# A changed prologue for a fused attention and expert kernel: scores first, block sums of v as products of their own, loads and splits in a new order

## The chip, the cores and the metric

The kernel runs on one core of a Trainium2 chip. The metric is the device time of one execution in microseconds, the median of several executions. TensorE (PE) multiplies matrices; its weight loads are listed as PEld. VectorE (DVE), ScalarE (ACT) and GpSimd (POOL) do elementwise work, and SyncE (SP) issues nearly all DMA transfers. Each engine takes its own instructions strictly in the order in which they were written.

## The reference

Three layers follow one another. The first is attention: 2 batches, 8 heads, 768 positions, head size 64. Each query sees the keys within 15 positions of itself and, beside them, 24 block keys, each the maximum over 32 keys; the value of a block is the mean of its 32 values.

```python
k_sum = k.reshape(B, H, nb, block, D).max(axis=3)
v_sum = v.reshape(B, H, nb, block, D).mean(axis=3)
scores_l = scale * np.matmul(q, k.transpose(0, 1, 3, 2))
scores_s = scale * np.einsum('bhsd,bhnd->bhsn', q, k_sum) + np.log(block)
scores_all = np.concatenate([np.where(mask_l, scores_l, -1e9), scores_s], axis=-1)
a = softmax(scores_all)
x = np.matmul(a, np.concatenate([v, v_sum], axis=2))
```

The second is a dense layer on 1536 tokens, `g = elu(x @ w_in)` and `x2 = g @ w_out`, with 512 and 2048 columns. The third is a top-1 mixture of 8 experts on `x2`, each with 512, 1024 and 512 columns and a limit on its number of tokens.

## The kernel before

The tokens are cut into four parts of 384 (`t` = 0 to 3, called NT). For attention a *pair* `p` is one part with two heads, 16 pairs in all, and a *unit* `u` is half a pair, 192 queries. The loop over `sl` writes one *slot* per unit; inside a slot the engines' work is written by hand, and that order is final, for there is no scheduler behind it. In slot `sl` the kernel writes the scores of unit `u = sl` (`pe_s`, tile S), the masked maximum (`dve_max`, custom DVE instructions on S), the exponential (`act_exp`), the division (`norm`: two small DVE instructions, L290 and L291, and a product on POOL), the transpose of unit `u-1` (`pe_t`, tile T), and the output of unit `u-2` (`pe_o`, tile O). Between them `busy(n)` writes n transposes of the identity matrix into an unused tile, called *fillers* here (tile `warm`).

The scores need the window keys `kw`. `prep_k` makes them from the loaded keys `kt`: two copies of key columns (the main one of 64 columns per window, the rest of 32), a maximum over blocks (`ks`, L195) and a copy of `ks`. The block sums of v are reduced on DVE from `vt` (`prep_va`, L209), transposed by PE (`pe_va`, tile V), scaled by ACT into `vs` (`fin_va`) and brought by a DMA of their own (`load_vs`) below the 96 window rows of `vw`, so that `pe_o` multiplies 120 rows at once. `pe_va` of the next pair is written before the scores of that pair.

Nine slots come before the dense layer sets in (`LAG` is 9). Slot 8 (`LAG - 1`) is a special one: it holds the scores of unit 8 and the first two products h0 and h1 of the first part with `w_in`, three of their four row blocks before the last outputs of attention are there and the fourth after them. Slots 9 to 16, called n = 0 to 7 here, each hold one attention unit of part 1 and one pair of products (tile h with `w_in`, tile acc with `w_out`) of part 0. For part 0 the weights are used as whole 32-bit numbers, put together by three DVE instructions each (`w_conv`, L399, L403, L406); for later parts they are split in two: `w_split` writes a rounded copy on ACT and the remainder on POOL (L413). `wpend` lists the splits that are due, `split_next()` takes one. From slot 18 on attention and the dense layer go on in another branch that the change does not touch. After the dense layer comes the routing to experts, and then the experts.

The sets `splits` (i0, i1, i2, o0, i3, o1, ... o7) and `corder` say in which order weights are loaded, put together and split. SP takes all loads from one list, and a load whose buffer is still in use holds up what stands behind it.

Of the kernel before, what the change touches and what calls it, by code (L numbers as in the profile page):

```python
# [9 lines left out]
F32 = mybir.dt.float32  # L10
# [10 lines left out]
P = 128  # L21
# [28 lines left out]
def build(tc, cap, qT, kT, vT, vP, wi, wo, wg, wgT, wx, out):  # L50
# [6 lines left out]
    with ctx:  # L57
# [111 lines left out]
        def load_vt(p):  # L169
            t, pr = divmod(p, NPAIR)  # L170
            if t % 2 == 0:
                if p == NPAIR - 1:
                    VT[p] = xpool.tile([P, NPAIR, S], F32, tag="xT2", name=f"vt{p}")[:, 0]
                else:
                    VT[p] = apool.tile([P, S], F32, tag="vt", bufs=1, name=f"vt{p}")
                nc.sync.dma_start(VT[p], vT[t // 2, pr])

        def load_vw(p):
            t, pr = divmod(p, NPAIR)
            b, half = divmod(t, 2)  # L180
            vw = apool.tile([P, QPT, P], F32, tag="vw", name=f"vw{p}")
            vbase = (b * (S + 2 * WIN) + half * TT) * DM + pr * P
            nc.sync.dma_start(
                vw[0:WK], bass.AP(vP.tensor, vbase, [[DM, WK], [QB * DM, QPT], [1, P]]))
            VW[p] = vw

        def prep_k(p):

            t, pr = divmod(p, NPAIR)
            kt = KT[p]  # L190
            kw = apool.tile([P, QPT, KEYS], F32, tag="kw", name=f"kw{p}")
            KW[p] = kw
            if t % 2 == 0:
                KS[p] = apool.tile([P, NSUM], F32, tag=f"ks{pr}", bufs=1, name=f"ks{p}")
                nc.vector.tensor_reduce(  # L195
                    out=KS[p], in_=kt[:, WIN : WIN + S].rearrange("p (u s) -> p u s", s=BLK),
                    op=ALU.max, axis=AX.X)
            else:
                KS[p] = KS[p - NPAIR]
            (nc.vector.tensor_copy if p >= 3 * NPAIR else nc.scalar.copy)(kw[:, :, 0:QB], kt[:, 0:TT].rearrange("p (i k) -> p i k", k=QB))  # L200
            rest = nc.gpsimd.tensor_copy if t == 0 and pr else nc.scalar.copy if t == 1 else nc.vector.tensor_copy
            rest(kw[:, :, QB:WK], kt[:, QB : QB + TT].rearrange("p (i k) -> p i k", k=QB)[:, :, 0 : WK - QB])
            (nc.gpsimd if t == 0 and pr else nc.vector).tensor_copy(
                out=kw[:, :, WK:KEYS], in_=KS[p].unsqueeze(1).to_broadcast([P, QPT, NSUM]))
# [21 lines left out]

        def load_vs(p):
            nc.sync.dma_start(
                out=VW[p][WK:KEYS], in_=VS[p][WK:KEYS].unsqueeze(1).to_broadcast([NSUM, QPT, P]))
# [75 lines left out]
        def pe_o(u):  # L305
            p, t, pr, g0 = where(u)
            po = PS["o", u] = psm(f"O{u}", "O")
            pT = PTS.pop(u)
            for gi in range(GRP):
                for hh in range(2):  # L310
                    nc.tensor.matmul(
                        po[hh * D : (hh + 1) * D, gi * QB : (gi + 1) * QB],
                        lhsT=VW[p][0:KEYS, g0 + gi, hh * D : (hh + 1) * D],
                        rhs=pT[0:KEYS, gi, hh * QB : (hh + 1) * QB], start=True, stop=True)

# [554 lines left out]
        load_k(0)  # L870
        load_q(0)
        load_vt(0)
        load_k(1)
        load_q(1)
        load_vw(0)
        prep_k(0)
        prep_va(0)
        pe_va(0)
        load_vt(1)
        load_vw(1)  # L880


# [51 lines left out]
        for sl in range(total):  # L934
# [16 lines left out]
            cv = list(corder.get(sl, ())) if sl >= LAG else []  # L951
            if 0 < n < FPG - 2:
                wpend.append(splits[n - 1])
            if FPG - 2 <= n <= FPG:
                wpend.extend(splits[2 * n - FPG + 1 : 2 * n - FPG + 3])
            if FPG < n < 2 * FPG - 2:
                wpend.append(splits[n + 2])

# [13 lines left out]
            if sl == LAG - 1:  # L972
# [4 lines left out]
                pe_o(u - 2)  # L977
                act_o(u - 2)
                w_conv([("i", 2)], (0, 1))
                pe_t(u - 1)  # L980
                mm1(0, 1, range(NCC - 1))
                w_conv([("i", 2)], (2,))
                w_prefetch()
                act_t(u - 1)
                pe_o(u - 1)
                act_o(u - 1)
# [3 lines left out]
                load_vs(p)  # L990
                load_k(p + 2)
                dve_max(u)
                elu_exp(0, 0)
                elu_max(0, 0)
                act_exp(u)
                prep_k(p + 1)
                norm(u)
                continue
# [157 lines left out]
            if u < NU:  # L1156
                pe_s(u)
            if sl < LAG - 1:
                busy(2 if sl < LAG - 3 else 4)
            if u - 2 in late:  # L1160
# [5 lines left out]
            if u < NU and sl % GPP == (p == 0):  # L1166
                fin_va(p)
                load_vs(p)
            if u < NU and sl % GPP == 0:
                if p + 2 < NPR:  # L1170
                    load_k(p + 2)
                if p + 2 == NPAIR - 1:
                    load_vt(p + 2)
            if u < NU and sl % GPP == 1 and p + 2 < NPR:
                load_q(p + 2)
            if u < NU and sl % GPP == 1 and p and p + 1 < NPR:
                load_vw(p + 1)
            if el:
                elu_exp(*el[1:])
            if u < NU:  # L1180
                dve_max(u)
                act_exp(u)

            if el:
# [3 lines left out]
            if dense:  # L1188
# [3 lines left out]
                split_next()  # L1192
                if n >= FPG - 2:
                    split_next()
                if sl % GPP and p + 1 < NPR:
# [12 lines left out]
            if u < NU and sl % GPP == 1 and p + 1 < NPR:  # L1208
                if not dense:
                    prep_va(p + 1)  # L1210
                if p + 2 < NPR and p + 2 != NPAIR - 1:
                    load_vt(p + 2)
            if sl < LAG and u - 2 in late:
                dve_o(u - 2)
            if u < NU and not dense:
                norm(u)
            if sl in (LAG - 3, LAG - 2):
                w_conv([("i", sl - LAG + 3)])
                w_prefetch()
# [16 lines left out]
            conv_next()  # L1236
            if sl in (LAG - 6, LAG - 5, LAG - 4, LAG - 3):
                w_prefetch()
            if sl < LAG - 1:
                busy(2 if sl < LAG - 3 else 4)  # L1240
            if 0 <= u - 1 < NU and u != NU:
# [115 lines left out]
        for v in range(3):  # L1357
            nc.vector.tensor_reduce(
                out=tabs[:, :, v].rearrange("p (k j) -> p k j", j=nj), in_=tmp[v], op=ALU.add, axis=AX.X)
            if v == 0:  # L1360
                by_rank(2)
        ysf = bpool.tile([P, DM], F32, tag="ys", bufs=3, name="ysf")
        busy(4)
        ahead(0, GRP)
        allsl = slots(tabs, NE * nj, "1")
        for k in range(1, NE):
            GS[k] = allsl + (k * nj,)
        finish(blk.y, st["slot0"][0][:, 0:1], st["slot0"][1][:, 0:1], "f", ysf)

# [105 lines left out]
def _layout(np, q, k, v, moe_w_in, moe_w_out, moe2_w_gate, moe2_w1, moe2_w2):  # L1475
# [4 lines left out]
    vT = v.reshape(NB, NPAIR, 2, S, D).transpose(0, 1, 2, 4, 3).reshape(NB, NPAIR, P, S)  # L1480
    vP = np.pad(v.transpose(0, 2, 1, 3).reshape(NB, S, DM), ((0, 0), (WIN, WIN), (0, 0)))
    wi = moe_w_in.reshape(NCC, P, NFC, P).transpose(2, 1, 0, 3).reshape(NFC, P, 512)
    wo = moe_w_out.reshape(NFC, P, DM)
# [24 lines left out]
```

## Time and profile before

| | before |
|---|---|
| median of 3 runs | 500.39 us (499.85 to 500.6) |
| the profiled execution, own time | 502.35 us |
| its span, first to last instruction | 500.6 us |
| PE busy | 473.9 us, 95% of the span |
| PEld, DVE, ACT, POOL busy | 394.3, 336.2, 265.3, 184.4 us |
| moved by DMA | 73.15 MB, mean 146 GB/s |
| DMA share in the first 44 us | 0.91 |

The profile shows one execution, with times from the start of its span. A busy PE isn't a PE at its peak, since matmuls are pipelined and their ends are modelled; so lengths of PE work are read here from the start of one group to the start of the next. [...] The chain of waits of this profile covers only the last microsecond, so the stretches are read from the order of time instead.

### The profile page before, as it was taken

The numbers are of one execution on the slowest core, as the hardware profiler recorded it, in microseconds if no ns is written. First come the engines' busy times: TensorE is split into PE (matmuls) and PEld (weight loads), VectorE is DVE, ScalarE is ACT, GpSimd is POOL, SyncE is SP. The second block draws the span as 40 slices with busy tenths as digits, with TensorE's granted clock in tenths as the row PEclk, the third lists the DMA queues.
The fourth block names the chain that finished last, engine by engine and source line by source line (L and its number), as shares of the span: only waits on it lengthen the run. The fifth ranks groups of instructions, "written<-read, shape, count | busy, mean of one in ns | idle before, by whom it ended". The sixth has DMA issues, their size and how long they took to land. (4 is left out here: it accounts for less than half of the span.)

```text
span 500.6 us, 9042 instructions
## 1 busy us (share of the span) xinstructions
PE 473.9 (95%) x2996; PEld 394.3 (79%) x2996; DVE 336.2 (67%) x887; ACT 265.3 (53%) x666; POOL 184.4 (37%) x189
## 2 busy tenths in 40 slices
PE   7999998899999999999999999999998999999892
PEld 6665555588888899998999999889768889888681
DVE  3778999866666557887179889747695855365560
ACT  3846556577665655564333333434735856476450
POOL 4412435665333347886333233122524030120340
PEclk8999999999999999999999999999999999999898
DMA  7898784332433253479010010105536875376470
GB/s 226 255 278 221 223 250 135 92 111 76 135 106 94 57 184 104 147 264 321 5 63 2 0 64 1 64 0 191 151 122 215 300 234 184 125 237 190 160 243 14
DMA packets 41890, 73.15 MB, mean 146 GB/s; under 512 B 4188, under 2 KB 18780, under 8 KB 41808
## 3 DMA queue, kind: packets, MB, share of 16 engines
q1 hardware_dynamic: 40048, 67.01, 43.2%
q0 software_dynamic: 1760, 5.19, 3.4%
q8 instruction: 34, 0.56, 0.5%
q14 instruction: 48, 0.39, 0.3%
HBM read 61.88 MB, written 9.70 MB: 143 GB/s over the span
## 5 line engine op out<-in xcount | busy, mean ns | idle before, releaser
L430 PE MATMUL h<-xT,Wi 128*128 128x384 f32 x672 | 130.2, 340 | 0.0
L475 PE MATMUL acc<-Wo,g 128*128 128x512 f32 x504 | 127.3, 396 | 0.6 <-POOL g L455 0.6
L430 PEld LDWEIGHTS h<-xT,Wi 128*128 128x128 f32 x672 | 118.0, 188 | 5.8 <-issue 1.9
L455 POOL TENSOR_TENSOR g<-e,g 128x384 fp32r<-128x384 f32 x55 | 65.0, 1182 | 131.5 <-ACT g L449 131.5
L475 PEld LDWEIGHTS acc<-Wo,g 128*128 128x128 f32 x504 | 92.8, 188 | 18.6 <-POOL g L455 1.4
L442 DVE SCALAR_TENSOR_TENSOR e<-e,h 128x384 f32<-128x384 f32 x64 | 35.3, 552 | 51.1 <-ACT e L438 48.8
L437 ACT ACTIVATE e<-h 128x384 f32<-128x384 f32 x64 | 31.5, 492 | 57.7 <-PE h L430 54.0
L667 DVE TENSOR_TENSOR E<-rawq,E 128x512 fp32r<-128x512 f32 x70 | 47.8, 723 | 9.6 <-ACT E L657 8.4
L449 ACT CAST g<-e 128x384 fp32r<-128x384 f32 x56 | 28.8, 514 | 45.7 <-DVE e L442 45.7
L284 ACT ACTIVATE sc<-sc,st 128x120 f32<-128x120 f32 x96 | 36.7, 385 | 20.1 <-DVE st L277 20.0
L799 PE MATMUL bh<-xbq,E 128*128 128x256 f32 (+1 forms) x288 | 43.6, 303 | 3.2 <-ACT ysf L703 1.3
L799 PEld LDWEIGHTS bh<-xbq,E 128*128 128x128 f32 x288 | 41.2, 188 | 5.5 <-issue 1.5
L657 ACT CAST E<-rawq 128x512 fp32r<-128x512 f32 x75 | 42.3, 617 | 4.5 <-issue 2.5
L292 POOL TENSOR_TENSOR sc<-sc,st 128x360 f32<-128x360 f32 x32 | 27.6, 862 | 43.6 <-DVE st L291 26.3
L788 PE MATMUL y<-E,g 128*128 128x512 f32 x168 | 41.7, 393 | 0.0
L537 DVE CUSTOM_DVE_ANT_0 dot<-a,wgb 128x512 f32<-128x512 f32 x48 | 40.0, 888 | 0.0
L788 PEld LDWEIGHTS y<-E,g 128*128 128x128 f32 x168 | 30.6, 188 | 5.7
L438 ACT ACTIVATE e<-e 128x384 f32<-128x384 f32 x64 | 33.6, 526 | 2.0
L277 DVE CUSTOM_DVE_ANT_0 sc<-S,masks 128x120 f32<-128x120 f32 x96 | 21.4, 277 | 17.9 <-PE S L252 11.0
L303 ACT COPY pT<-T 120x384 f32<-120x384 f32 x32 | 15.3, 480 | 26.8 <-PE T L299 25.5
L807 DVE TENSOR_TENSOR g<-e,g 128x256 fp32r<-128x256 f32 (+1 forms) x24 | 11.3, 470 | 24.7 <-ACT g L806 24.7
L704 POOL DMA_INDIRECT out<-ys,sidx x6 | 6.3, 1051 | 48.0 <-ACT ys L703 46.5
(249 smaller groups left out, 702.0 us busy)
## 6 DMA issues: line engine op xcount, KB each, us to landing
rawq<-wx SPq DMA_DIRECT2D x88, 256.0 KB, 3.7
rawi<-wi SPq DMA_DIRECT2D x16, 512.0 KB, 6.4
rawo<-wo SPq DMA_DIRECT2D x16, 512.0 KB, 4.3
vw<-vP SPq DMA_DIRECT2D x16, 288.0 KB, 4.1
kt<-kT SPq DMA_DIRECT2D x8, 400.0 KB, 5.4
qt<-qT SPq DMA_DIRECT2D x16, 192.0 KB, 4.2
vt<-vT SPq DMA_DIRECT2D x8, 384.0 KB, 3.2
out<-xg SPq DMA_DIRECT2D x12, 256.0 KB, 4.4
```

The source lines that it names most:

```text
L284: nc.scalar.activation(out=sc[:, gi], in_=sc[:, gi], func=AF.Exp, bias=st[:, 0, gi : gi + 1], scale=-1.0, accum_out=st[:, 1, gi : gi + 1])
L430: nc.tensor.matmul(HP[t, f][:, 0:TT], lhsT=w[:, s, c * P : (c + 1) * P], rhs=xT[t][:, xs, c, :], start=c == 0 and n == 0, stop=c == NCC - ...
L437: nc.scalar.activation(out=e, in_=HP[t, f][:, 0:TT], func=AF.Exp)
L438: nc.scalar.activation(out=e, in_=e, func=AF.Relu, bias=1.0, scale=-1.0)
L442: nc.vector.scalar_tensor_tensor(out=e, in0=e, scalar=-1.0, in1=h[:, 0:TT], op0=ALU.mult, op1=ALU.max)
L455: eng.tensor_tensor(g[:, 1], EP.pop((t, f)), g[:, 0].bitcast(F32), op=ALU.subtract)
L475: nc.tensor.matmul(accp[tb], lhsT=g[:, s, tb * P : (tb + 1) * P], rhs=w[:, ws], start=f % FPG == 0 and n == 0, stop=f % FPG == FPG - 1 and ...
L537: nc.vector.tensor_tensor_reduce(out=junk, in0=x2[t * BPT + tb], in1=WGB[e // 2][:, e % 2], scale=1.0, scalar=0.0, op0=ALU.mult, op1=ALU.a ...
L657: (nc.vector.tensor_copy if m in vec else nc.scalar.copy)(EW[k][m][:, 0], raw_of(k, m))
L667: (nc.gpsimd if m in pool else nc.vector).tensor_tensor(w[:, 1], raw, w[:, 0].bitcast(F32), op=ALU.subtract)
L788: nc.tensor.matmul(ys[b], lhsT=g[:, s, b * P : (b + 1) * P], rhs=w[:, ws], start=f == 0 and n == 0, stop=f == 7 and n == 2)
L799: nc.tensor.matmul(h[:, 0:nt], lhsT=EW[k][half * NCC + c][:, ws, fc * P : (fc + 1) * P], rhs=xb[:, s, c, 0:nt], start=n == 0, stop=n == 3 ...
```

## The change

The program differs in eight places. The scores of pair 0 no longer stand behind the transpose of its block sums: `prep_va(0)` and `pe_va(0)` move into slots 0 and 1. For part 0 the block sums become two products of their own (24 rows, 192 columns) that open each sum in `pe_o`, and the DMA `load_vs` falls away there. `vw` is loaded from a host layout with one row of 3 KB per key instead of six of 512 bytes. The loads of keys, queries and values are issued in another order, and v of pairs 1 to 3 gets buffers of its own. The main key copies of pairs 1 to 3 move from ACT to POOL. Fillers become fewer. In slot 8 the maximum, exponential and division of unit 8 move ahead of h1. The splits are taken one per slot through n = 7 and two in n = 8 and 9. Near the end, `finish` of the first expert block moves ahead of four fillers.

```diff
@@ load_vw @@
-            vbase = (b * (S + 2 * WIN) + half * TT) * DM + pr * P
-            nc.sync.dma_start(
-                vw[0:WK], bass.AP(vP.tensor, vbase, [[DM, WK], [QB * DM, QPT], [1, P]]))
+            nc.sync.dma_start(vw[0:WK], vP[b, half, pr])
@@ prep_k @@
-            (nc.vector.tensor_copy if p >= 3 * NPAIR else nc.scalar.copy)(kw[:, :, 0:QB], kt[:, 0:TT].rearrange("p (i k) -> p i k", k=QB))
+            main = nc.gpsimd.tensor_copy if t == 0 and pr else nc.vector.tensor_copy if t == 3 else nc.scalar.copy
+            main(kw[:, :, 0:QB], kt[:, 0:TT].rearrange("p (i k) -> p i k", k=QB))
@@ load_vs @@
+            if p < NPAIR:
+                return
@@ pe_o @@
+            own = KEYS if t else WK
+            if t == 0:
+                for hh in range(2):
+                    nc.tensor.matmul(
+                        po[hh * D : (hh + 1) * D, 0 : GRP * QB],
+                        lhsT=VS[p][WK:KEYS, hh * D : (hh + 1) * D],
+                        rhs=pT[WK:KEYS, :, hh * QB : (hh + 1) * QB], start=True, stop=False)
...
-                        lhsT=VW[p][0:KEYS, g0 + gi, hh * D : (hh + 1) * D],
-                        rhs=pT[0:KEYS, gi, hh * QB : (hh + 1) * QB], start=True, stop=True)
+                        lhsT=VW[p][0:own, g0 + gi, hh * D : (hh + 1) * D],
+                        rhs=pT[0:own, gi, hh * QB : (hh + 1) * QB], start=t > 0, stop=t > 0 or gi == GRP - 1)
@@ before the loop @@
         load_k(0)
         load_q(0)
+        prep_k(0)
+        load_k(1)
         load_vt(0)
-        load_k(1)
+        load_vw(0)
         load_q(1)
-        load_vw(0)
-        prep_k(0)
-        prep_va(0)
-        pe_va(0)
         load_vt(1)
-        load_vw(1)
+        load_k(2)
@@ the splits that are due @@
-            if 0 < n < FPG - 2:
+            if 0 < n < FPG:
                 wpend.append(splits[n - 1])
-            if FPG - 2 <= n <= FPG:
-                wpend.extend(splits[2 * n - FPG + 1 : 2 * n - FPG + 3])
-            if FPG < n < 2 * FPG - 2:
-                wpend.append(splits[n + 2])
+            if FPG <= n < FPG + 2:
+                wpend.extend(splits[2 * n - FPG - 1 : 2 * n - FPG + 1])
+            if FPG + 2 <= n < 2 * FPG - 1:
+                wpend.append(splits[n + 1])
...
-                if n >= FPG - 2:
-                    split_next()
@@ slot 8 @@
+                dve_max(u)
                 w_conv([("i", 2)], (0, 1))
...
+                act_exp(u)
+                norm(u)
                 pe_o(u - 1)
...
-                load_k(p + 2)
-                dve_max(u)
                 elu_exp(0, 0)
                 elu_max(0, 0)
-                act_exp(u)
                 prep_k(p + 1)
-                norm(u)
@@ slots 0 to 7 @@
+            if sl == 1:
+                pe_va(0)
             if sl < LAG - 1:
-                busy(2 if sl < LAG - 3 else 4)
+                busy(1 if sl < LAG - 3 else 2)
...
+            if sl < LAG - 1 and sl % GPP == 1:
+                load_k(p + 3)
+                if p + 3 < NPAIR:
+                    load_vt(p + 3)
...
+            if sl == 0:
+                prep_va(0)
+            if sl in (LAG - 3, LAG - 2):
+                w_conv([("i", sl - LAG + 3)], (0, 1))
...
-            if sl < LAG - 1:
-                busy(2 if sl < LAG - 3 else 4)
+            if LAG - 3 <= sl < LAG - 1:
+                busy(2)
@@ first expert block @@
+        finish(blk.y, st["slot0"][0][:, 0:1], st["slot0"][1][:, 0:1], "f", ysf)
         busy(4)
         ahead(0, GRP)
...
-        finish(blk.y, st["slot0"][0][:, 0:1], st["slot0"][1][:, 0:1], "f", ysf)
```

On PE the start of the program stood thus before (a name's number tells one buffer from another; `x24` merges equal instructions; S is a unit's scores, V a transposed block sum, T a transposed unit, O an output):

```order
L867 MATMUL warm<-ident 128x128 x24
L217 MATMUL V_176<-ident,va_126 120x128
L263 MATMUL S_182<-kw_169,qt_159 64x120 x6
L867 MATMUL warm<-ident 128x128 x4
L263 MATMUL S_214<-kw_169,qt_159 64x120 x6
L867 MATMUL warm<-ident 128x128 x4
L299 MATMUL T_246<-ident,sc_194 120x128 x3
L217 MATMUL V_250<-ident,va_128 120x128
L263 MATMUL S_252<-kw_202,qt_165 64x120 x6
L867 MATMUL warm<-ident 128x128 x2
L311 MATMUL O_264<-pT_262,vw_167 64x64 x6
```

In the changed program the same stretch reads:

```order
L877 MATMUL warm<-ident 128x128 x24
L266 MATMUL S_179<-kw_161,qt_159 64x120 x6
L877 MATMUL warm<-ident 128x128
L266 MATMUL S_209<-kw_161,qt_159 64x120 x6
L218 MATMUL V_216<-ident,va_126 120x128
L877 MATMUL warm<-ident 128x128
L302 MATMUL T_239<-ident,sc_188 120x128 x3
L218 MATMUL V_243<-ident,va_128 120x128
L266 MATMUL S_245<-kw_197,qt_173 64x120 x6
L877 MATMUL warm<-ident 128x128
L315 MATMUL O_256<-pT_254,vs_220 64x192 x2
L321 MATMUL O_256<-pT_254,vw_171 64x64 x6
```

The first V now stands behind the scores of units 0 and 1; the second V still stands ahead of the scores of unit 2; each output has two products of 192 columns more.

On DVE the start of the changed program reads as follows (`ks` is a block maximum of keys, `va` a block sum of v, the ISA rows on `sc` are a unit's maximum and those on `st` alone its read-out; unit 0 is `sc_188`, unit 1 `sc_227`):

```order
L280 ISA st_189 128x1
L210 TENSOR_REDUCE va_126<-vt_169 128x24
L195 TENSOR_REDUCE ks_198<-kt_167 128x24
L293 TENSOR_SCALAR st_189<-st_189 128x3
L294 RECIPROCAL st_189<-st_189 128x3
L280 ISA sc_227,st_228<-S_209,masks 128x120
L280 ISA st_228 128x1
L280 ISA sc_227,st_228<-S_209,masks 128x120
L280 ISA st_228 128x1
L280 ISA sc_227,st_228<-S_209,masks 128x120
L280 ISA st_228 128x1
L210 TENSOR_REDUCE va_128<-vt_175 128x24
```

The first block sum moved from ahead of the first maximum to behind it, so that from there two sums, a key maximum, a division and a maximum stand in one row ahead of the second V.

On POOL slots n = 5 to n = 8 stood thus before (a row on `sc` is a unit's division and comes once a slot, a row on `Wi` or `Wo` is a split):

```order
L413 TENSOR_TENSOR Wi_964<-T_493,Wi_964 128x512
L292 TENSOR_TENSOR sc_954<-sc_954,st_955 128x360
L413 TENSOR_TENSOR Wo_1025<-T_493,Wo_1025 128x512
L413 TENSOR_TENSOR Wi_1028<-T_494,Wi_1028 128x512
L292 TENSOR_TENSOR sc_1015<-sc_1015,st_1016 128x360
L413 TENSOR_TENSOR Wo_1084<-T_494,Wo_1084 128x512
L413 TENSOR_TENSOR Wi_1087<-T_495,Wi_1087 128x512
L292 TENSOR_TENSOR sc_1074<-sc_1074,st_1075 128x360
L413 TENSOR_TENSOR Wo_1126<-T_495,Wo_1126 128x512
L292 TENSOR_TENSOR sc_1133<-sc_1133,st_1134 128x360
L413 TENSOR_TENSOR Wi_1158<-T_496,Wi_1158 128x512
```

In the changed program they read:

```order
L423 TENSOR_TENSOR Wi_942<-T_463,Wi_942 128x512
L295 TENSOR_TENSOR sc_932<-sc_932,st_933 128x360
L423 TENSOR_TENSOR Wo_1003<-T_463,Wo_1003 128x512
L295 TENSOR_TENSOR sc_993<-sc_993,st_994 128x360
L423 TENSOR_TENSOR Wi_1059<-T_464,Wi_1059 128x512
L295 TENSOR_TENSOR sc_1049<-sc_1049,st_1050 128x360
L423 TENSOR_TENSOR Wo_1098<-T_464,Wo_1098 128x512
L295 TENSOR_TENSOR sc_1105<-sc_1105,st_1106 128x360
L423 TENSOR_TENSOR Wi_1130<-T_465,Wi_1130 128x512
```

Slots n = 6 and n = 7 have one split each instead of two, and the two that moved stand in later slots.

## Rows read from the trace of the kernel before

**Rows 1.** Busy time per stretch (windows): stretch, length, each engine's busy us, PEclk, DMA, GB/s.

```profile
100.00:200.00 100.00, 100.00 (x784) 87.82 (x783) 62.92 (x192) 64.12 (x185) 45.66 (x43) 1.00 0.36 109
```

**Rows 2.** Waits of PE over the span: who, for whom, us in total, times, longest.

```profile
PE acc L471 <- DVE x L406: 2.6, 2, 1.5
PE O L311 <- DMA vw<-vs: 0.5, 1, 0.5
PE acc L471 <- DVE T L406: 0.2, 1, 0.2
```

**Rows 3.** Timeline of the start: start us, length us, engine, line, operation, [idle <-releaser].

```profile
1.75 4.35 PE L867 MATMUL warm<-ident 128*128 128x128 f32 x24 [1.75 <-POOL ident masks.py:199]
...
5.10 0.34 DVE L203 COPY kw<-ks 128x144 f32<-128x144 f32 x1
...
8.31 1.46 PE L263 MATMUL S<-kw,qt 64*64 64x120 f32 x12
...
8.57 0.34 POOL L202 COPY kw<-kt 128x192 f32<-128x192 f32 x1 [3.00 <-DMA kt<-kT]
...
11.42 0.17 DVE L290 TENSOR_SCALAR st<-st 128x3 f32<-128x3 f32 x1
...
12.08 0.28 DVE L277 CUSTOM_DVE_ANT_0 sc<-S,masks 128x120 f32<-128x120 f32 x1 [0.28 <-PE S L263]
...
12.69 0.95 DVE L209 TENSOR_REDUCE va<-vt 128x24 f32<-128x768 f32 x1
```

**Rows 4.** Busy time per stretch, 6 to 8 and 8 to 12 us.

```profile
6.00:8.00 2.00, 0.10 (x1) 0.00 (x0) 0.95 (x1) 0.00 (x0) 0.00 (x0) 1.00 1.05 331
8.00:12.00 4.00, 3.95 (x30) 3.03 (x30) 1.91 (x9) 1.83 (x8) 0.70 (x3) 0.57 0.91 227
```

**Rows 5.** Timeline of PE, slot of unit 2, from its scores to those of unit 3.

```profile
13.95 0.83 PE L263 MATMUL S<-kw,qt 64*64 64x120 f32 x12
...
14.71 0.44 PE L867 MATMUL warm<-ident 128*128 128x128 f32 x2
...
15.08 0.57 PE L311 MATMUL O<-pT,vw 120*64 120x64 f32 x12
...
15.58 0.44 PE L867 MATMUL warm<-ident 128*128 128x128 f32 x2
...
15.85 0.49 PE L299 MATMUL T<-ident,sc 128*120 128x128 f32 x3
...
16.27 0.83 PE L263 MATMUL S<-kw,qt 64*64 64x120 f32 x12
```

**Rows 6.** Timeline, slots of units 5 and 6.

```profile
23.20 0.95 DVE L209 TENSOR_REDUCE va<-vt 128x24 f32<-128x768 f32 x1
...
24.46 0.83 PE L263 MATMUL S<-kw,qt 64*64 64x120 f32 x12
...
26.42 0.57 PE L311 MATMUL O<-pT,vw 120*64 120x64 f32 x12 [0.55 <-DMA vw<-vs]
```

**Rows 7.** Groups of PE, 1.7 to 4.9 us, then 4.9 to 6.2: count | busy us, mean ns.

```profile
L867 PE MATMUL warm<-ident 128*128 128x128 f32 x15 | 3.4, 418 | 1.8 <-POOL ident masks.py:199 1.8
L867 PE MATMUL warm<-ident 128*128 128x128 f32 x11 | 1.5, 291 | 0.0
```

**Rows 8.** Timeline of POOL and DVE, slots n = 6 and n = 7.

```profile
82.78 1.72 POOL L413 TENSOR_TENSOR Wi<-T,Wi 128x512 fp32r<-128x512 f32 x1
83.29 1.23 DVE L290 TENSOR_SCALAR st<-st 128x3 f32<-128x3 f32 x1
84.66 0.66 DVE L406 SCALAR_TENSOR_TENSOR x<-rawo,x 128x512 uint32<-128x512 uint32 x1
...
89.27 1.63 DVE L406 SCALAR_TENSOR_TENSOR x<-rawo,x 128x512 uint32<-128x512 uint32 x1
```

**Rows 9.** Timeline of PE near the end: two groups of 18 equal products.

```profile
464.39 6.00 PE L725 MATMUL bh<-E,xbq 128*128 128x512 f32 x18 [1.97 <-issue]
...
479.23 4.37 PE L725 MATMUL bh_0z<-E,xbq 128*128 128x512 f32 x18
```

More of the change, by code (lines that the diff above doesn't have):

```diff
@@ L171, in load_vt @@
             if t % 2 == 0:
-                if p == NPAIR - 1:
-                    VT[p] = xpool.tile([P, NPAIR, S], F32, tag="xT2", name=f"vt{p}")[:, 0]
+                if 0 < p < NPAIR:
+                    if p == 1:
+                        VT["early"] = xpool.tile([P, NPAIR, S], F32, tag="xT2", name="vt1")
+                    VT[p] = VT["early"][:, p]
                 else:
@@ L1168, in build @@
                 load_vs(p)
[L1169 to L1173, printed above, removed]
+            if sl >= LAG and u < NU and sl % GPP == 0 and p + 2 < NPR:
+                load_k(p + 2)
+            if u < NU and sl % GPP == 1 and p and p + 1 < NPR:
+                load_vw(p + 1)
             if u < NU and sl % GPP == 1 and p + 2 < NPR:
                 load_q(p + 2)
-            if u < NU and sl % GPP == 1 and p and p + 1 < NPR:
-                load_vw(p + 1)
+            if sl < LAG - 1 and sl % GPP == 1:
+                load_k(p + 3)
+                if p + 3 < NPAIR:
+                    load_vt(p + 3)
             if el:
@@ L1210, in build @@
                     prep_va(p + 1)
-                if p + 2 < NPR and p + 2 != NPAIR - 1:
+                if NPAIR <= p + 2 < NPR:
                     load_vt(p + 2)
+            if sl == 0:
+                load_vt(2)
+                load_vw(1)
             if sl < LAG and u - 2 in late:
@@ L1217, in build @@
             if sl in (LAG - 3, LAG - 2):
-                w_conv([("i", sl - LAG + 3)])
+                w_conv([("i", sl - LAG + 3)], (2,))
                 w_prefetch()
@@ L1236, in build @@
             conv_next()
-            if sl in (LAG - 6, LAG - 5, LAG - 4, LAG - 3):
+            if sl in (LAG - 7, LAG - 5, LAG - 4, LAG - 3):
                 w_prefetch()
-            if sl < LAG - 1:
-                busy(2 if sl < LAG - 3 else 4)
+            if LAG - 3 <= sl < LAG - 1:
+                busy(2)
             if 0 <= u - 1 < NU and u != NU:
@@ L1481, in _layout @@
     vP = np.pad(v.transpose(0, 2, 1, 3).reshape(NB, S, DM), ((0, 0), (WIN, WIN), (0, 0)))
+    vP = np.stack([vP[:, i * QB : i * QB + WK] for i in range(NQB)], axis=2)
+    vP = vP.reshape(NB, WK, 2, QPT, NPAIR, P).transpose(0, 2, 4, 1, 3, 5)
     wi = moe_w_in.reshape(NCC, P, NFC, P).transpose(2, 1, 0, 3).reshape(NFC, P, 512)
```

## The prediction

> **What bounds the kernel now.** I read the busy time per stretch first, then the waits of PE, then the order of time in the first 45 us and around 80 us. From 100 to 200 us PE is busy without a break [rows 1], so whatever the first 100 us win or lose arrives whole at the end. The question is therefore when PE gets through the prologue. Its waits name two places [rows 2]: 2.6 us in two waits for put-together weights (DVE, L406), and 0.5 us for the DMA that brings block sums. DMA engines are 0.91 busy [rows 4], yet hardly anything on PE waits for them, so bytes saved are worth little by themselves. What sets the pace of the nine attention slots is order. In a slot with even number PE itself is full, 2.32 us from scores to scores: scores 0.76, two fillers 0.37, output 0.50, two fillers 0.27, transpose 0.42 [rows 5]. In a slot with odd number DVE's chain is longer: scores, maximum, block sum of v, transpose V, and only then the next scores. In slot 5 the sum runs from 23.20 for 0.95 us and the scores of unit 6 follow at 24.46, 0.31 behind its end [rows 6].
>
> **The change part by part.** The sum is made against the profiled execution's own 502.35 us; the median shown is 500.39, 1.96 lower, and I carry the difference over unchanged.
>
> *Scores first.* The keys of pair 0 are ready at 5.10 + 0.34 = 5.44 and the 24 opening fillers end near 1.75 + 4.35 = 6.1 [rows 3], so unit 0's scores start at about 6.1 instead of 8.31, 2.2 us sooner. That lead doesn't last. The next V still stands ahead of unit 2's scores, and DVE comes to it through a row of five. The first v now lands in the place that the second keys had; these were there at 8.57 [rows 3]. From there: block sum 0.95, key maximum 0.95 (an equal reduction), division 0.35 (the 0.17 of L290 twice), maximum 12.69 - 12.08 = 0.61, second sum 0.95 [rows 3], which ends at 12.38. With the 0.31 from above, unit 2's scores start at 12.7 instead of 13.95 [rows 5]: -1.25. Bounds: 0, if v lands a microsecond later, and -2.2, if the whole lead is kept.
>
> *The idle time that this makes.* Between about 8.5 and 11.8 PE has only V and one filler. Before, it did 0.10 us of work from 6 to 8, and the granted clock was 0.57 from 8 to 12, although PE was 3.95 of 4.00 us busy there [rows 4]: 4 x 0.43 = 1.7 us of full clock lost. Now the idle time is later and longer, so I expect as much of half clock from about 11.7 on, over unit 2's scores, its output and the transpose. Half clock costs these scores 1.46 - 0.83 = 0.63 [rows 3, 5]; with part of the output I take +1.0, with bounds 0 and 1.7. Unit 3's scores then start at 16.0, against 16.27.
>
> *Fillers and block sums.* In slots 0 to 5 one filler remains of four: 0.64 becomes about 0.17, -0.47. In slots 6 and 7 four remain of eight; at 1.5/11, less the last one's tail, some 0.11 each [rows 7], that is -0.44. The two new products per output are run in two passes each like the others (the scores' six appear as 12): 4 x 192 = 768 columns. The nearest rows: scores pass 12 x 120 = 1440 columns in 0.76, outputs 12 x 64 = 768 in 0.50 [rows 5], so 0.41 by the one and 0.50 by the other; the scores without their starting gap would give some 0.31. I take 0.40, nearest to the scores, and keep 0.31 and 0.50. Where PE sets the pace this gives slot 4 -0.07, slot 6 -0.04, slot 7 -0.04. Slot 6 also loses the wait of 0.55 for the block sums' DMA [rows 6], since there is no such DMA for part 0; nothing is late behind it, the transposed unit having waited already. Slots 3 and 5 stay as they are, by DVE's chain. Together -0.70.
>
> *Slot 8.* Two outputs take 2 x 0.40 more on PE, which is the bound through h0 and h1. Moving unit 8's maximum and division ahead takes DVE work out of the stretch behind h0, and the 0.17 for which acc waited there [rows 2] goes. +0.63. So the first acc comes 1.25 - 1.0 + 0.70 - 0.63 = 0.3 us sooner than before.
>
> *The order of splits.* In slot n = 6 a second split runs on POOL from 82.78 to 84.50, and beside it the tiny L290 takes 1.23 instead of 0.17; in n = 7 L406 at 89.27 takes 1.63 instead of 0.66 [rows 3, 8]. Both stand on DVE's way to the weight for which acc waits. With one split per slot these delays go: 1.06 + 0.97 = 2.03 of the 2.6 us waited [rows 2]. The splits land in slots n = 8 to 14, where DVE puts no weights together for part 0. Bounds: -2.6, all the waits, and 0, if PE waits there instead.
>
> *At nothing:* 3-KB rows, the order of loads, main key copies on POOL and `finish` earlier. The cover of the loads is the lead that only the first v and the 0.55 of slot 6 lack; if it were gone, a late load costs its lateness, as it did there. POOL waits 3.00 us even for its first key copy [rows 3]; a main copy there, twice the columns of the 0.34, is about 0.7 per pair, and the idle time of POOL covers it. ACT is relieved by three copies but is waited for by none of the chains above.
>
> Sum: -1.25 + 1.0 - 0.70 + 0.63 - 2.03 = -2.35. So 502.35 - 2.35 = 500.0 for an execution like the profiled one, and 498.0 as median.
>
> Fewer fillers matter only through the clock, and here the trace speaks. The first 15 fillers have a mean length of 418 ns, the next 11 of 291 ns [rows 7], and PE had done nothing but these transposes before its clock rose. [...]
>
> **The rivals.**
>
> First, the prologue wins more. If the idle time doesn't bring the clock down, because enough of V, filler and scores falls into it, the +1.0 goes: 497.0. For it speaks that the clock stayed at 1.00 from 6 to 8 itself with hardly any work, so the fall comes late and may meet work that matters less. Against it: the idle time is longer than before.
>
> Second, the gain of the splits only moves. Slots n = 8 and 9 hold two splits, and the slot after n = 8 has one more than before between two divisions and the remainder that acc needs there. Then the 2.03 go and 500.0 is left, no change. Against it: from 100 us on PE has no idle time at all [rows 1], so there is room.
>
> Third, slower: the clock. PE is relieved of 26 fillers in slots 0 to 7 and waits in every odd slot for DVE's chain. If that makes its clock fall again in the slots, each such stretch loses up to 1.7 us of full clock [rows 4], as PE is near its bound there. One more stretch leaves the kernel faster or equal (499.7), two more give 501.4, three 498.0 + 5.1 = 503.1. It decides from the second. I price it at 502.3. Against it: with the block sums' products PE has about as much to do per slot as before.
>
> Fourth, POOL's longer key copies hold up DVE. The same row of 1.23 us shows that a POOL operation can hold a DVE operation until it ends [rows 8]. Three pairs with copies of 0.7 + 0.34 beside a division or copy on DVE's chain cost up to 3 x 1.0: 501.0. Against it: the copies stand behind the division of the odd unit, when DVE takes a maximum or reduces, and the reductions shown keep to 0.95 [rows 3, 6].
> [...]
>
> Fifth, the end. 18 products at 464.39 take 6.00 us, after PE stood still for 1.97, and 18 equal ones at 479.23 take 4.37 [rows 9]; the difference of 1.63 is the clock. A program shifted by two microseconds may meet that fall differently: 496.4.
>
> **How the numbers follow.** Chances: forecast (498.0) 0.45; clock kept (497.0) 0.16; splits win nothing (500.0) 0.18; clock falls again (502.3) 0.08; POOL holds DVE (501.0) 0.07; the end (496.4) 0.06. A measurement of this kernel tells a change from none from about 0.2%, 1.0 us: 499.39 and 501.39 are the borders. Faster: 0.41 of the forecast's 0.45 (its own range is 496.6 to 499.6 by the bounds of products and splits), the 0.16, 0.02 of the splits' case and the 0.06, together 0.65. Slower: the 0.08 and 0.03 of POOL's case, 0.11. Same: the rest, 0.24. The range of 8 in 10 is 495.9 to 500.7: below it lies the sum of all lower bounds, above it most of the two cases that lose.
>
> **What would show it.** Right: unit 0's scores near 6.1, unit 2's near 12.7 and the clock at half somewhere between 8 and 15; unit 8's scores about 1.0 us sooner; the first acc about 0.3 us sooner; the 2.6 us in which acc waits for DVE down to some 0.6; L290 at 0.17 in n = 6 and L406 at 0.66 in n = 7. Wrong: an output that waits for `vs`, a maximum that waits for keys or v, granted clock under 1.00 between 16 and 30 us, or PE waiting for POOL's remainders in the slots behind n = 8.

## The result, and the profile after

The changed kernel takes 508.56 us (median of 5 runs, 506.32 to 510.81); the kernel before, run beside it, takes 500.0 (498.97 to 500.6). The ratio is 1.0149, with a 95% interval of 1.0104 to 1.0194: slower. The profiled execution has a span of 508.9 us and a time of its own of 510.58, against 500.6 and 502.35. Ratios here and below leave out runs that lie over 1.5% above the fastest of their kernel; medians and ranges keep them.

The busy time per stretch shows the loss at once. Columns as in [rows 1]: stretch, length, busy time of PE, PEld, DVE, ACT and POOL, granted clock as a share (0.50 is called half clock), DMA share, GB/s.

```profile
8.00:12.00 4.00, 1.45 (x16) 1.02 (x17) 3.68 (x17) 2.49 (x12) 1.10 (x2) 1.00 1.05 343
13.00:37.00 24.00, 24.00 (x177) 15.59 (x175) 11.11 (x55) 12.01 (x48) 6.93 (x12) 0.50 0.67 208
100.00:200.00 100.00, 98.87 (x807) 86.16 (x806) 64.29 (x200) 66.45 (x195) 45.74 (x44) 1.00 0.38 112
```

From 8 to 12 us PE works 1.45 of 4.00 us; before it was 3.95 [rows 4]. From 13 to 37 us it is busy all the time, at half clock. By the clock records of the trace, half clock lasts from 13.14 to 37.04 us, 23.9 us; in the profile of before it lasted 3.4, from 8.30 to 11.72. Every run of the changed kernel has a mean clock between 0.965 and 0.974; the profile of before has 0.989.

The timeline of PE (start, length, line, operation, idle time before it) has the standstill and the slots behind it:

```profile
6.73 0.83 PE L266 MATMUL S<-kw,qt 64*64 64x120 f32 x12
8.58 0.83 PE L266 MATMUL S<-kw,qt 64*64 64x120 f32 x12 [0.75 <-DVE st L280]
9.88 0.27 PE L877 MATMUL warm<-ident 128*128 128x128 f32 x1
11.81 0.54 PE L302 MATMUL T<-ident,sc 128*120 128x128 f32 x3 [1.66 <-POOL sc L295]
12.57 0.95 PE L266 MATMUL S<-kw,qt 64*64 64x120 f32 x12
...
16.36 1.47 PE L266 MATMUL S<-kw,qt 64*64 64x120 f32 x12
17.75 0.47 PE L877 MATMUL warm<-ident 128*128 128x128 f32 x1
18.16 0.90 PE L315 MATMUL O<-pT,vs 24*64 24x192 f32 x4
18.99 0.91 PE L321 MATMUL O<-pT,vw 96*64 96x64 f32 x12
19.83 0.90 PE L302 MATMUL T<-ident,sc 128*120 128x128 f32 x3
20.52 0.42 PE L218 MATMUL V<-ident,va 128*120 128x128 f32 x1
20.87 1.47 PE L266 MATMUL S<-kw,qt 64*64 64x120 f32 x12
...
38.48 0.83 PE L266 MATMUL S<-kw,qt 64*64 64x120 f32 x12
39.25 2.20 PE L433 MATMUL h<-x,T 128*128 128x384 f32 x6
41.38 0.54 PE L315 MATMUL O<-pT,vs 24*64 24x192 f32 x4
41.85 0.57 PE L321 MATMUL O<-pT,vw 96*64 96x64 f32 x12
...
53.22 2.84 PE L481 MATMUL acc<-T,e 128*128 128x512 f32 x6
...
92.87 2.84 PE L481 MATMUL acc<-x,e 128*128 128x512 f32 x6 [0.41 <-DVE x L416]
...
99.76 2.66 PE L440 MATMUL h<-xT,Wi 128*128 128x384 f32 x12
```

Slot 3 takes 4.51 us (16.36 to 20.87), where scores of 0.83 [rows 5] take 1.47. Laid beside before, the lag is: unit 2's scores -1.38 (12.57, before 13.95), unit 3's +0.09, unit 8's +7.88 (38.48, before 30.60), the first acc +8.58 (53.22, before 44.64), the first h of part 1 +6.53 (99.76, before 93.23), the end +8.3. So five slots lose 7.8 us, slot 8 and the stretch up to the first acc 0.7 more, and the new order of splits gives back 2.05 before 100 us. Past 360 us, where the lag stands at 6.24 (the product into bh0f, 360.89, before 354.65), two more are lost; there the profile has another half clock (385.2 to 388.6), and two branches, treated below, wait 0.5 us longer. The three starts of before are:

```profile
30.60 0.83 PE L263 MATMUL S<-kw,qt 64*64 64x120 f32 x12
...
44.64 2.84 PE L471 MATMUL acc<-T,e 128*128 128x512 f32 x6 [0.17 <-DVE T L406]
...
93.23 2.67 PE L430 MATMUL h<-xT,Wi 128*128 128x384 f32 x12
```

The waits of PE (who, for whom, us, times, longest) show what the splits gave, against 2.6 us in [rows 2]; the DMA of block sums is gone from the list:

```profile
PE T L302 <- POOL sc L295: 1.7, 1, 1.7
PE S L266 <- DVE st L280: 0.8, 1, 0.8
PE acc L481 <- DVE x L416: 0.6, 2, 0.4
```

The equal rows to [rows 8], n = 6 and 7 on POOL and DVE:

```profile
90.13 1.27 POOL L423 TENSOR_TENSOR Wo<-T,Wo 128x512 fp32r<-128x512 f32 x1 [3.96 <-ACT Wo L422]
95.09 1.52 POOL L423 TENSOR_TENSOR Wi<-T,Wi 128x512 fp32r<-128x512 f32 x1 [1.63 <-ACT Wi L422]
```

```profile
91.87 0.15 DVE L293 TENSOR_SCALAR st<-st 128x3 f32<-128x3 f32 x1
92.15 0.66 DVE L416 SCALAR_TENSOR_TENSOR x<-rawo,x 128x512 uint32<-128x512 uint32 x1
95.40 1.23 DVE L293 TENSOR_SCALAR st<-st 128x3 f32<-128x3 f32 x1
96.77 0.66 DVE L416 SCALAR_TENSOR_TENSOR x<-rawo,x 128x512 uint32<-128x512 uint32 x1
```

In n = 6 the tiny instruction is down from 1.23 us to 0.15. In n = 7 it still takes 1.23, behind the one split that is left there (it ends at 96.61), as it did before, in a row that [rows 8] leaves out:

```profile
87.90 1.24 DVE L290 TENSOR_SCALAR st<-st 128x3 f32<-128x3 f32 x1
```

What went in n = 7 is the second split, and with it the 1.63 us of L406 (now L416, 0.66); acc waits 0.18 there, before 1.15.

### The profile page after: what moved, and what is told of

Read it like the earlier page. It is cut to its first block, busy times and chain, and to the rows that moved or that the text cites. A ratio compares the mean times of both kernels' runs of the same rounds, so it can differ in the third digit from the quotient of the medians.

```text
span 508.9 us, 9037 instructions
## 1 busy us (share of the span) xinstructions
PE 484.9 (95%) x3002; PEld 400.3 (79%) x3002; DVE 334.2 (66%) x887; ACT 264.3 (52%) x663; POOL 186.5 (37%) x192
## 5 line engine op out<-in xcount | busy, mean ns | idle before, releaser
L809 PE MATMUL bh<-xbq,E 128*128 128x256 f32 (+1 forms) x288 | 45.1, 310 | 3.5 <-issue 1.4
L809 PEld LDWEIGHTS bh<-xbq,E 128*128 128x128 f32 x288 | 42.7, 196 | 5.8 <-issue 1.8
```

The lines of the kernel that those rows point to most:

```text
L809: nc.tensor.matmul(h[:, 0:nt], lhsT=EW[k][half * NCC + c][:, ws, fc * P : (fc + 1) * P], rhs=xb[:, s, c, 0:nt], start=n == 0, stop=n == 3 ...
```

## The experiments

The theory after the result: the 1.66 us in which PE waits for unit 0's division set off the half clock. Rivals: the fillers left out of the later slots, and the products of 24 rows. "Half" below is the half clock of the prologue, by the clock records of the profiled execution; the mean clocks of all runs, where given, cover the whole span. The edits are shortened, and the remark behind a `#` says where a line stands.

**All fillers back.**

```diff
-busy(1 if sl < LAG - 3 else 2)      # ahead of the output
+busy(2 if sl < LAG - 3 else 4)
-if LAG - 3 <= sl < LAG - 1: busy(2) # ahead of the transpose
+if sl < LAG - 1: busy(2 if sl < LAG - 3 else 4)
```

> The changed kernel with the 26 fillers of before put back (2 and 2 in slots 0 to 5, 4 and 4 in slots 6 and 7). Theory FILLERS: the clock falls near 13 us as in the changed kernel, where it stayed at half from 13.2 to 37.0, but with the fillers it comes back after a few us as in the kernel before (8.3 to 11.7); unit 8's scores near 31, time 499 to 502. Theory IDLE (the length hangs on the idle time before it, 2.7 us of 7.8 to 11.8, not on the fillers): half clock as long as in the changed kernel, and the fillers make it longer, time 508 to 513. Theory PRODUCTS (the two products of 24 rows per output keep the clock low): like IDLE, 508 to 513.

508.41 us, ratio 1.0124 (1.0087 to 1.0161). Half from 13.86 to 24.1: 10.2 us instead of 23.9, unit 8's scores at 35.09. The fillers shorten it, as the first theory has it, and not in this profile alone: the four runs have mean clocks of 0.976 to 0.989, the changed kernel's at most 0.974. The time is what the other two theories have. Part of the reason stands in the waits near the end, at two branches:

```profile
PE bh L735 <- issue: 4.8, 1, 4.8
PE bh L809 <- issue: 3.3, 1, 3.3
```

The changed kernel waits 2.2 and 1.4 there, before 2.0 and 1.1 ([rows 9] has the first): 4.5 us more, 400 us behind the prologue. This run's time alone would have been read wrongly.

**The idle time filled in both places.**

```diff
-busy(1 if sl < LAG - 3 else 2)
+busy((8, 16)[sl] if sl < 2 else 1 if sl < LAG - 3 else 2)
```

> The changed kernel with 7 more fillers in slot 0 and 15 more in slot 1, put where PE stood still for 0.75 us (7.8 to 8.6) and 1.66 us (10.1 to 11.8); slots 2 to 7 keep the changed kernel's one or four fillers. Theory IDLE: no fall at 13, the slots run at full clock, unit 8's scores at 27.5 to 29 instead of 38.5, time 495 to 499. Theory FILLERS: the later slots have too little work of the kind that keeps the clock, so it falls a few us later and stays; unit 8's scores at 33 to 38, time 503 to 509. Theory PRODUCTS: like FILLERS.

No half clock in the prologue; unit 8's scores at 28.87, first acc at 43.61, first h of part 1 at 90.14, 3.09 us ahead of before. So the trigger is the idle time. The time missed its expectation: 503.9, ratio 1.0055 (1.003 to 1.0081), with 6.3 us of waiting at the two branches and a half clock at the first of them (436.76 to 440.17) that the changed kernel's profile doesn't have.

**Which idle time.** Only slot 1 filled, and only slot 0:

```diff
+busy(16 if sl == 1 else 1 if sl < LAG - 3 else 2)   # slot 1
+busy(8 if sl == 0 else 1 if sl < LAG - 3 else 2)    # slot 0
```

> The changed kernel with the 15 fillers of slot 1 alone (in the 1.66 us before 11.8); the 0.75 us of slot 0 stay idle. If the 1.66 us set off the fall: no half clock in the prologue, first acc near 43.6 as with both places filled, time 499.5 to 501.5 (3017 instructions, waits at the branches 3 to 3.5). If both stretches are needed for it or the first alone sets it off: half clock of 7 us or more from 13, first acc 47 or later, time 503 to 509.

> The changed kernel with the 7 fillers of slot 0 alone (in the 0.75 us before 8.6); the 1.66 us of slot 1 stay idle. If the 1.66 us set off the fall: half clock from about 13 for 15 us and more, first acc 49 to 53, time 505 to 509. If it takes both: no fall, first acc near 43.6, time 499 to 501.5.

Slot 1: 499.6 us, ratio 0.9942 (0.9916 to 0.9967), first acc at 44.06. Its timeline and stretches:

```profile
10.16 1.91 PE L877 MATMUL warm<-ident 128*128 128x128 f32 x16
12.09 0.55 PE L302 MATMUL T<-ident,sc 128*120 128x128 f32 x3
...
12.86 0.83 PE L266 MATMUL S<-kw,qt 64*64 64x120 f32 x12
...
29.32 0.83 PE L266 MATMUL S<-kw,qt 64*64 64x120 f32 x12
...
44.06 2.84 PE L481 MATMUL acc<-T,e 128*128 128x512 f32 x6
```

```profile
8.00:12.00 4.00, 2.84 (x29) 2.47 (x29) 3.25 (x15) 2.11 (x11) 1.06 (x2) 1.00 1.05 324
13.00:37.00 24.00, 23.34 (x259) 14.94 (x257) 15.69 (x70) 15.27 (x63) 8.93 (x14) 1.00 0.91 292
```

Slot 0: 508.57 us, ratio 1.0085 (1.0045 to 1.0125), half from 12.88 to 43.6, first acc at 56.78. The same stretches:

```profile
8.00:12.00 4.00, 1.71 (x19) 1.04 (x16) 3.07 (x15) 1.94 (x10) 1.01 (x3) 1.00 1.04 315
13.00:37.00 24.00, 24.00 (x178) 15.93 (x177) 10.53 (x49) 12.03 (x46) 7.09 (x12) 0.50 0.65 192
```

Fifteen transposes of nothing, in time that was idle, decide between 0.50 and 1.00 from 13 to 37 us: 259 matmuls fit in where 178 did. These two runs differ in transposes only, by 9 us of median (499.6 and 508.57): with the 15 in slot 1 the granted clock stayed at 1.00. The ten runs with slot 0 filled lie between 502.93 and 511.77, mean clocks 0.982 to 0.964: the length differs from run to run. The ten with slot 1 filled have 0.989 to 0.995, so the two kernels differ in every run and not in their profiles alone.

**No fillers in the later slots.**

```diff
+busy((8, 16)[sl] if sl < 2 else 0)   # and none ahead of the transpose
```

> The changed kernel with 8 and 16 fillers in slots 0 and 1 and none in slots 2 to 7. Theory IDLE: no fall, unit 8's scores at 27.5 to 28.5 (28.87 with fillers), first acc 42.5 to 43.3; theory CODE (below) gives 3.1 to 3.6 us of waiting without a releaser at the two branches near 435 and 463, and so 500 to 501.5. Theory FILLERS (slots without fillers lose the clock): a fall of 7 us or more between 14 and 35, unit 8's scores after 31, time 503 to 509.

499.4 us, ratio 0.9959 (0.9927 to 0.999); no half clock from 0 to 460 us, unit 8's scores at 28.39, first acc at 43.12, 0.9 and 1.8 us at the branches. As a trigger the missing fillers are refuted: without the idle time this profile needs none of them. Two of the ten runs have mean clocks of 0.984 and 0.985, below all with slot 1 filled; where those ran at half clock isn't shown.

**What makes it last.** First, no products of their own:

```diff
-if p < NPAIR: return                    # in load_vs
-own = KEYS if t else WK                 # in pe_o; its two products out
+own = KEYS
```

> The changed kernel with the block sums of part 0 brought by their DMA again, as before, and no products of their own; fillers as in the changed kernel. Theory PRODUCTS (the products of 24 rows keep the clock at half from 13 to 37): the half clock ends after 3 to 7 us, unit 8's scores near 31, time 499 to 503. Theory IDLE with FILLERS (the idle time before 12 us starts the fall, too few fillers keep it): half clock of 15 us and more, but each slot shorter by the 0.83 us that the products take at half clock; unit 8's scores at 33 to 36, time 503 to 507.

499.75 us, ratio 0.9962 (0.9939 to 0.9985), half from 12.85 to 19.68, unit 8's scores at 31.42. That is what the theory of the products forecast, with the reserve that PE stood still inside that stretch (1.47 us) for the block sums' DMA. Two more runs, one with 2 and 2 fillers in slots 2 to 7 and all products, one with the changed kernel's fillers and products for pair 0 alone:

```diff
+busy(1 if sl < 2 else 2)                        # and busy(2) ahead of the transpose from slot 2
```
```diff
+if p == 0: return                               # in load_vs
+own = KEYS if p else WK                         # in pe_o, products if p == 0
```

> The changed kernel with 2 and 2 fillers in slots 2 to 7 (12 more in all), and 1 each in slots 0 and 1 as it has, so that the idle 1.66 us stay. 3014 matmul instructions, so the waits at the two branches should stay near 3.3 us. Theory LENGTH BY FILLERS: the fall comes at 13 and ends by 25, as with all fillers back (10.2 us), instead of after 23.9 and 30.7 us in the two profiles with the changed kernel's own; time 501 to 504.5. Theory LENGTH BY PRODUCTS alone: half clock of 20 us and more, time 506 to 512.

> The changed kernel with its fillers and its idle time in slot 1, but products of their own for pair 0 alone; block sums of pairs 1 to 3 by DMA. Theory LENGTH BY PRODUCTS: the fall comes at 13 and ends after 7 to 11 us, first acc at 44 to 46.5, time 499 to 503. Theory LENGTH BY FILLERS alone: half clock of 20 us and more, first acc at 49 to 52, time 504 to 509.

Half lasted 13.65 us in both (12.19 to 25.84 and 12.51 to 26.16), first acc at 50.70 and 47.68. 504.61 us against 502.06, ratio 1.0023 (0.9978 to 1.0067), and 501.62, ratio 0.9992 (0.9956 to 1.0029). Both answers hold in part: each change alone shortens the stretch to about half, and neither alone to the 3.4 us of before. Since the length differs from run to run, single profiles are thin evidence; the medians of the mean clocks agree, with 0.969 for the changed kernel and with slot 0 filled, 0.9825 and 0.982 for these two, 0.986 without products and 0.993 with slot 1 filled. What fillers and fewer products have in common for the clock is not shown.

Nor does the standstill set off the fall every time. One of the ten runs with 2 and 2 fillers took 498.32 us at a mean clock of 0.995. As an estimate from these, that is 5.0 us of half clock in all (496.6 x 0.005 x 2); the profiled run of the same kernel spends 4.1 at its end alone, so hardly any is left for the prologue.

**Both mended at once.** Slots 0 and 1 filled, no products at all:

> The changed kernel without own products, and with the idle time of slots 0 and 1 filled (8 and 16 fillers, as in the run that filled it). Theory IDLE: no fall in the prologue; slots of even number 0.47 shorter, slot 8 8.28 us as before instead of 9.2, first acc near 41.5 (43.61 with products, 43.36 in the kernel before with the new splits and no fall), first h of part 1 near 88; faster than all so far, a ratio to before of 0.991 to 0.995. Rival: an output waits for the block sums' DMA in several slots, first acc 43 or later, ratio 0.997 to 1.002.

499.94 us, ratio 0.996 (0.9938 to 0.9983), first acc at 45.43: the rival came, with a ratio between the two forecasts. The output of unit 0 waits 2.45 us for the late DMA of its block sums, and half clock follows that standstill (16.36 to 19.77). The row names ACT, which had ended 1 us earlier; that it is the DMA is borne out by the next kernel, where products for pair 0 take this wait away:

```profile
13.52 0.33 PE L875 MATMUL warm<-ident 128*128 128x128 f32 x1
16.30 0.89 PE L319 MATMUL O<-pT,vw 120*64 120x64 f32 x12 [2.45 <-ACT sc L285]
```

So the next kernel keeps products for pair 0 (the edit of pair 0 above), fills slots 0 and 1 with 8 and 16, and has no other filler:

> The changed kernel with 8 and 16 fillers in slots 0 and 1, none in slots 2 to 7, and products of their own for the block sums of pair 0 alone; those of pairs 1 to 3 come by the DMA as before. Without any product the output of unit 0 waited 2.5 us and more for that DMA; with products in all outputs slot 8 took 9.2 us instead of 8.3. Theory IDLE: no fall in the prologue, first acc at 41.5 to 42.3 (43.12 with products everywhere), first h of part 1 at 88.0 to 88.9, a ratio to before of 0.990 to 0.995. Rival: the outputs of units 2, 4 or 6 wait for the DMA instead, first acc at 42.6 or later, ratio 0.995 to 0.999.

498.35 us, ratio 0.9928 (0.9896 to 0.996); no half clock before 461 us, first acc at 42.36, first h of part 1 at 88.91. It is faster than the kernel before, and its ratio is the lowest here, though the interval overlaps that of slot 1 filled; the changed kernel's lies wholly above 1. The first acc is 0.06 later than expected; outputs still wait 2.2 us for `pT` and 0.3 for the DMA.

**Parts alone, on the kernel before.** The new number of fillers:

> The kernel before with the changed kernel's number of fillers alone (14 instead of 40). Theory FILLERS: the fall at 8.3 us lasts longer than its 3.4 us of before, by 10 us and more, and the time is 504 to 509. Theories IDLE and PRODUCTS: the fall stays at 3.4 us, slots a little shorter, time 499 to 500.5.

503.02 us, ratio 1.0021 (0.9974 to 1.0068): unclear, and neither forecast came. Half didn't come at 8.3 at all but from 24.75 to 31.58, behind waits of 0.88 and 0.75 us in unit 5's slot. The six runs lie between 499.32 and 506.52.

The new order of splits:

> The kernel before with the new order of splits alone. Forecast of the prediction: the waits of acc for put-together weights in slots n = 6 and 7 fall from 2.6 to some 0.6 us and the time by 2.0, to 498.0. Rival of the prediction: the gain only moves, 500.0. In the changed kernel the lag behind before shrank from 8.58 us (first acc) to 6.53 us (first h of part 1) and stood at 6.24 at 361 us, which speaks for 497.7.

500.48 against 501.39, ratio 0.998 (0.9957 to 1.0002). In the trace the step is there: from the first acc to the first h of part 1 46.54 us (43.36 to 89.90) instead of 48.59, that is -2.05, and

```profile
PE acc L471 <- DVE x L406: 0.6, 2, 0.4
```

The time alone does not separate -2.0 from 0. This profile has no half clock in the prologue, and unit 2's scores at 12.65 with the old order. The two profiles of the next experiment, whose prologue is that of before, have none either. So the fall at 8.3, from which the prediction took its price, stands in one of four profiles of that prologue. In that one PE stood still for 1.95 us ahead of the first V, in the others for 1.26, 1.44 and 0.39.

**The waits at the branches.** 16 and 32 fillers more ahead of the first expert, where PE waits anyway:

```diff
-busy(4)
+busy(20)     # the other: busy(36)
 ahead(0, GRP)
```

> The kernel before with 16 more fillers ahead of the first expert, near 375 us, where PE waits 1.3 us anyway. It tests why the run with the fillers back and the run with the idle time filled waited 8.1 and 6.4 us, without a releaser, for the first products behind two branches near 440 and 465, where the kernel before waits 3.1 and the changed kernel 3.5. Theory CODE: the length hangs on how many instructions TensorE has ahead of the branch (about 80, 60 and 28 for fillers and products in the kernels with 3.1 to 3.5 us, 104 and 112 in the two others); here 112, so 6 to 8 us and a time of before plus 3.5 to 5.5. Theory TRAFFIC: it hangs on the transfers that happen to run then; here 3.1 as before, time of before plus 0.5 to 1.0.

> The kernel before with 32 more fillers ahead of the first expert (16 more left the two waits without a releaser at 1.2 and 1.8 us). By the profiles' count of TensorE's matmul instructions, builds with 2970 to 3012 wait 2.7 to 3.5 us at the two branches, those with 3024 and 3028 wait 6.4 and 8.1; this one has 3028. Theory CODE PLACE (the place of the code behind the branch in the stream decides): 6 to 8 us of waiting, time of before plus 5 to 7 (2.3 of it the fillers). Theory TRAFFIC: 3 us of waiting as before, time of before plus 1.5 to 2.5.

With 16: 501.35 us, ratio 0.9993 (0.9965 to 1.002), waits of 1.2 and 1.8; the number of instructions as first counted (112) is refuted. With 32: 507.47 us, ratio 1.0134 (1.0081 to 1.0186), as the theory of the place has it, but the one profile, the fastest of its four runs, shows only 3.0 and 1.4 us. The other three have mean clocks of 0.984 to 0.988 against its 0.996; what cost them their time no trace shows:

```profile
PE bh L799 <- issue: 3.0, 1, 3.0
PE bh L725 <- issue: 1.4, 1, 1.4
```

Open, then: all builds with at most 3017 matmul instructions, by the profiles' count, wait 2.6 to 3.6 us at the two branches together, the three with 3024 and 3028 wait 6.3, 8.1 and 4.4. The profiles name no engine and no transfer that ends these waits; what they wait for isn't shown.

## Why the prediction was wrong

It gave 498.0 with 495.9 to 500.7, and 508.56 came. The step that failed is the price of the clock: the term +1.0 in "The idle time that this makes", and the same price in the third rival. The sign of being wrong that the prediction named, a granted clock under 1.00 between 16 and 30 us, came.

*The idle time.* That PE would stand still between 8.5 and 11.8, and that the clock would fall behind it, came true: 1.66 and 0.75 us of waiting, half from 13.14 (predicted 11.7). The term was +1.0 with bounds 0 and 1.7, because I took the one fall in the profile of before, 3.4 us long, as the size of every fall. It lasted 23.9. With slot 1 filled the same program needs 16.46 us from unit 2's to unit 8's scores (12.86 to 29.32), the changed kernel 25.91 (12.57 to 38.48): the term was 9.4. The 8.4 beyond +1.0 and the 2.0 lost past 360 us are nearly all of the miss (10.6).

*The third rival* came nearest, with a chance of 0.08: the clock falls, and PE is near its bound. It counted stretches of 1.7 us loss each and stopped at three. The argument against it, that the products give PE as much to do per slot as before, was wrong in kind: PE was busy 24.00 of 24.00 us and the clock stayed at half. Nor did it take repeated waits. With slot 0 filled, two waits in slot 1 (0.93 and 1.66 us) were followed by none from 13 to 43 us, and half clock lasted 30.7; where PE sets the pace the slots stretch with it (slot 3 takes 4.51 us in the changed kernel and 2.86, 15.32 to 18.18, with slot 1 filled).

*Scores first.* Unit 0's at 6.73 (predicted 6.1; the opening fillers ran to 6.8), unit 2's at 12.57 (predicted 12.7). But the gain of 1.25 was read against an execution whose clock had fallen at 8.3. Where the old order runs without that fall, in four profiles, unit 2's scores come at 12.39 to 13.07; with the changed order, in eleven, at 12.41 to 13.38. The order as such gives nothing that these tell from zero, and that -1.38 came for -1.25 is owed to the profile it was read against.

*Fillers and products.* An output's products take 0.47 us at full clock (41.38 to 41.85), within 0.31 to 0.50; at half 0.83. With 0.40 taken, slot 4 was to be 0.07 shorter than 2.32; at full clock it takes 2.47 (18.18 to 20.65, slot 1 filled). The 0.55 of slot 6 went, nothing was late behind it. From unit 3's to unit 8's scores it is 14.00 (15.32 to 29.32) against 14.33 (16.27 to 30.60): -0.33, where -0.70 was summed. That the clock rose during the opening fillers, as the prediction has it, the clock records don't show: they have 1.00 from 1.75 to 4.85 us, where a filler took 418 ns, as from 4.85 to 6.20, where it took 291 [rows 7].

*Slot 8.* From unit 8's scores to unit 9's 9.22 instead of 8.28, +0.94 for two outputs; the rest up to the first acc -0.24 (5.52, before 5.76). Together +0.70, predicted +0.63.

*The order of splits.* -2.05, predicted -2.03; waits of 0.6, as forecast. The second rival is refuted in the trace as far as 360 us, where the lag stands at 6.24 after 6.53; in the time of that part alone it is not settled. The forecast's own range, 496.6 to 499.6, doesn't follow from the bounds that it names: those of products and splits give some 497.0 to 500.5.

*The other rivals.* The first, a clock that is kept, gave 497.0; with slot 1 filled it is kept, and the ratio of 0.9942 puts 500.0 to 497.1. The fourth fell: no division waited for a key copy. The fifth fell too: the 18 products behind the standstill, at 472.62, still take 5.99 us, [rows 9] has 6.00.

*At nothing.* POOL's key copies took 0.50 instead of 0.7 and held nobody; no maximum waited for keys or v after the first slots. `finish` changed nothing: its place in the waits is taken by the tables (DVE, L1373), 1.3 us for the 1.3 of before.

So the sum was wrong for the clock. Without the +1.0 it is -3.35, and with slot 1 filled, at full clock, the same change gives a ratio of 0.9942, about -2.9 us. That this is near is in part luck. The splits give their -2.05, but the changed prologue without a fall has its first acc at 44.06 and 43.61 (slot 1 and both slots filled), and the old one without a fall at 43.36, 43.99 and 44.21: it gains nothing that these tell from zero. What the rest of the -2.9 comes from is not shown; falls that the kernel before has in some of its runs may be part of it.

## What to carry to other kernels

Price an idle stretch of TensorE by what runs behind it at half clock until the clock comes back, not by the one fall that a profile happens to show; in a prologue of narrow products that was 9 us for 1.66. Fill such a stretch where it lies (15 fillers in idle time left unit 2's scores at 12.86, in the changed kernel 12.57, and saved 9 us of median) before thinning work elsewhere. And read gains against an execution that is undisturbed at that place: the gain of a new order may be the clock of the old profile. One profile doesn't tell how long half clock lasts in other runs; the mean clock of every run does so roughly (0.964 to 0.982 in the ten with slot 0 filled).

## What was not expected of the hardware

- Half clock outlasted full activity: from 13 to 37 us PE was busy 24.00 of 24.00 us at 0.50. With these small products half clock lasted 23.9 us, and 30.7 with slot 0 filled. Busy is the profile's measure here; what the clock goes by isn't shown.
- One program varies: with slot 0 filled ten runs spread over 8.8 us, with slot 1 filled over 4.1 (497.76 to 501.9).
- Waits at two branches that nothing in the trace releases grew from 3.6 us (the changed kernel) to 8.1 in a build that differs only by fillers 400 us earlier.
